# Attention into a two-layer MLP on one core: the start of the program in a written order of its own, with earlier weight loads

## The chip, the cores and the metric

One NeuronCore of a Trainium2 chip runs the whole program. The metric is the device time of one execution in microseconds (us). The kernel before takes 985.35 us (median of 3 runs, 983.48 to 986.13).

## The reference

Local-global attention over 8 batches and 8 heads (512 local and 32 global tokens, head size 64), then an MLP on every token. All in float32:

```python
s_g  = scale * q_g @ [k_g, k_l].T          # global queries see everything
s_l  = [scale * q_l @ k_g.T,               # local queries: the global keys
        where(|i - j| <= 32, scale * q_l @ k_l.T, -1e9)]   # and a band of 32
attn = concat(softmax(s_g) @ [v_g, v_l], softmax(s_l) @ [v_g, v_l])
x    = attn, heads side by side            # 4352 tokens x 512
out  = (max(x @ w_in, 0) ** 2) @ w_out     # 512 -> 2048 -> 512
```

The weights are used in two ways. The first MLP block multiplies in plain float32, with weights whose words are put together on chip ("wf"). All later blocks multiply three times with faster operands, each value split in a high and a low part ("ws").

## The kernel before

**Work.** Attention goes by pairs of heads: 64 pairs, pair `q` holding two heads (index `x` = 0, 1) of half a batch. Four pairs give the 256 tokens of one MLP block; there are 17 blocks of 8 steps each. The main loop (L506) counts `t`. Even `t` handles pair `q = t//2`; from `t = LAG = 9` on, every `t` also handles step `m = t - 9` of the MLP. So the first four pairs (`t` = 0 to 8) run before any MLP step: they are called the prelude here, and `t` = 9 to 16 the first MLP block.

**One pair.** `load_raw` brings queries and keys (128 x 960 words, 480 KB), `load_v` the values of two pairs (512 KB in the prelude), each by one SP DMA. `scores` and `g_scores` are 12 matmuls into the PSUM tile `s`. `softmax1` (DVE) takes masked score and maximum, `softmax2` (ACT) the exponential, `softmax3` (DVE) the division. `turn` copies the result on POOL into 16-bit `planes[x]` and has SP transpose it by DMA into `turned[x]`; `join` (POOL) makes float32 words of it in `joined[x]`. `av` multiplies by the values into `xa`, `x_evac` copies that to `xg` (first four pairs) or `x_h`. `g_evac` copies the scores of the global queries from `s` to `sg`: four DVE copies a pair.

**One MLP step.** `gemm1` writes `h`, `act1` squares its positive part, `gemm2` of the step before adds into `o`.

**Weights.** 32 chunks `wr` of 512 KB come by SP DMA (`w_load`). `w_abs` (ACT) and two DVE operations (`w_bits`) make `wf` of each; `w_split` (ACT, DVE) makes `ws`. `PLAN` says per `t`, at four places of the step, how many half-chunks of bits (`b`) and splits (`s`) are issued. A chunk's load is issued by `w_start` at most `LOOK = 2` chunks ahead.

**What sets the order.** Up to `t` = 16 a scheduler may move instructions on each engine (`FREE = (17, ...)`, L508; PE is kept up to `t` = 8 too). From `t` = 17 each engine runs its instructions in the order in which the code issues them. Weight, global-value and second mask loads are always free (`nc.sync`). An engine's queue is in order on the chip: an instruction that waits holds all behind it.

Of the kernel before, what the change touches and what calls it, by code (L numbers as in the profile page):

```python
# [7 lines left out]
F32 = mybir.dt.float32  # L8
# [9 lines left out]
P = 128  # L18
# [11 lines left out]
LAG = 9  # L30
NEARLY = 8

PLAN = [",,,b", "b,,,b", "b,,,b", "b,,b,", "b,,b,", "b,,b,", "b,,b,", "b,b,,b", "b,b,,b", "bb,bb,bb,bb", "bb,bb,bb,bb", "bbs,bb,bbs,bbs", "bbs,bbs,bbs,bbs", "bbs,bbs,bbs,bbs", "bbs,bbs,bs,s", "s,s,s,", "s,s,s,", "s,s,s,", "s,s,,", "s,s,,", "s,s,,", "s,s,,", "s,s,,"]
FREE = (17, 17, 17, 17, 17)
LOOK = 2
WCH = 32


# [21 lines left out]
def attention_moe(  # L60
# [19 lines left out]
    pairs = {}  # L80

    w_bufs = {"free": WCH}

    def w_take(n):
        w_bufs["free"] -= n
# [16 lines left out]
    def load_v(q):  # L102
        if q < NEARLY:
            w_take(1)
            v = wp.tile([P, 2, 512], F32, tag="w", name=f"v{q}")
            sp.dma_start(v, pk[q : q + 2, :, VO:PK].rearrange("t p n -> p t n"))
            for i in range(2):
                pairs[q + i]["v"] = v[:, i, :]
        else:
            v = pairs[q]["v"] = p2.tile([P, 512], F32, tag="v", name=f"v{q}")  # L110
            sp.dma_start(v, pk[q, :, VO:PK])

    masks = cp.tile([P, 4 * WN], F32, name="masks")
    load_raw(0)
    load_raw(1)
    load_raw(2)
    load_v(0)
    load_raw(3)

    x_h = cp.tile([P, 2, 4, HALF], F32R, name="x_h")  # L120
    x_l = cp.tile([P, 2, 4, HALF], F32R, name="x_l")
# [1 line left out]
    xg0 = cp.tile([P, 4, SG], F32, name="xg0")  # L123
    sg = cp.tile([P, 2, 544], F32, name="sg")
    planes = [cp.tile([P, 768], U16, name=f"planes{i}") for i in range(2)]
    turned = [cp.tile([P, 6, P], U16, name=f"turned{i}") for i in range(2)]
    joined = [cp.tile([P, 384], F32, name=f"joined{i}") for i in range(2)]
    gp = cp.tile([P, 1280], U16, name="gp")
    gpt = cp.tile([P, 640], F32, name="gpt")
# [3 lines left out]

    def scores(q):
        pr = pairs[q]
        bank = pr["s"] = ps_a.tile([P, 2, 512], F32, tag="s", name=f"s{q}")
        raw = pr["raw"]
        for w_ in range(4):
            u, c = divmod(w_, 2)
            k = KO + WN * w_ + 32 * (w_ == 3)  # L140
            for x in range(2):
                r = slice(64 * x, 64 * x + 64)
                pe.matmul(
                    bank[64 * c : 64 * c + 64, x, WN * u : WN * u + WN],
                    raw[r, QO + 64 * w_ : QO + 64 * w_ + 64],
                    raw[r, k : k + WN],
                    start=True,
                    stop=True,
                    skip_group_check=True,
                )  # L150
# [7 lines left out]
    def g_scores(q):  # L158
        pr = pairs[q]
        bank, raw = pr["s"], pr["raw"]  # L160
        for c, (k, n, _) in enumerate(g_parts(q)):
            for x in range(2):
                r = slice(64 * x, 64 * x + 64)
                pe.matmul(
                    bank[64 * c : 64 * c + 64, x, 2 * WN : 2 * WN + n],
                    raw[r, 0:64],
                    raw[r, k : k + n],
                    start=True,
                    stop=True,
                    skip_group_check=True,  # L170
                )
        if q < NEARLY:
            w_take(-1)

    def g_evac(q):
        bank, grp = pairs[q]["s"], (q // 2) % 2
        for c, (_, n, o) in enumerate(g_parts(q)):
            for x in range(2):
                r = 64 * (q % 2) + 32 * x
                ve.tensor_copy(sg[r : r + 32, grp, o : o + n], bank[64 * c : 64 * c + 32, x, 2 * WN : 2 * WN + n])  # L180

    def softmax1(q, x):
        pr = pairs[q]
        hf = (q // 4) % 2
        if x == 0:
            pr["prob"] = p2.tile([P, 2, 2, WN], F32, tag="prob", name=f"prob{q}")
        st = pr["st", x] = p2.tile([P, 8], F32, tag=f"st{x}", name=f"st{q}_{x}")
        for u in range(2):
            m = 2 * hf + u
            ve.tensor_tensor_reduce(  # L190
                out=pr["prob"][:, x, u, :],
                in0=pr["s"][:, x, WN * u : WN * u + WN],
                in1=masks[:, WN * m : WN * m + WN],
                scale=-0.125,
                scalar=3.0e38,
                op0=ALU.add,
                op1=ALU.min,
                accum_out=st[:, u : u + 1],
            )

    def softmax2(q, x):
        pr = pairs[q]
        st, sums = pr["st", x], pr["s"][:, x, 3 * WN : 3 * WN + 2]
        for u in range(2):
            p_ = pr["prob"][:, x, u, :]
            ac.activation(out=p_, in_=p_, func=AF.Exp, scale=-1.0, bias=st[:, u : u + 1], accum_out=sums[:, u : u + 1])

    def softmax3(q, x):
        pr = pairs[q]
        st, sums = pr["st", x], pr["s"][:, x, 3 * WN : 3 * WN + 2]  # L210
        ve.tensor_scalar(out=st[:, 6:8], in0=sums, scalar1=1e-9, scalar2=None, op0=ALU.add)
        ve.reciprocal(out=st[:, 2:4], in_=st[:, 6:8])
        for u in range(2):
            p_ = pr["prob"][:, x, u, :]
            ve.tensor_scalar(out=p_, in0=p_, scalar1=st[:, 2 + u : 3 + u], scalar2=None, op0=ALU.mult)

    def turn(q, x):

        words = pairs[q]["prob"][:, x].bitcast(U16)
        to = planes[x].rearrange("p (h k u n) -> p h k u n", h=2, k=3, u=2)  # L220
        for h in range(2):
            src = words[:, :, 64 + h :: 2].rearrange("p u (k n) -> p k u n", k=2)
            po.tensor_copy(to[:, h, 0:2, :, :], src)
        src = words[:, :, :64].rearrange("p u (n h) -> p h u n", h=2)
        po.tensor_copy(to[:, :, 2, :, 0:32], src)
        sp.dma_start_transpose(out=turned[x], in_=planes[x])

    def join(q, x):
        words = joined[x].bitcast(U16).rearrange("p (n h) -> p h n", h=2)
        po.tensor_copy(words, turned[x].rearrange("p (h c) n -> p h (c n)", h=2))  # L230

    def xa_tile(q):
        return ps_a.tile([P, 2, 512], F32, tag="xa", name=f"xa{q}")
# [70 lines left out]

    def g_load_v(b, grp, pair):
        gv = state["gv"] = p1.tile([P, 5, P], F32, tag="gv", name=f"gv{b}_{grp}_{pair}")
        nc.sync.dma_start(gv, vg[b, 2 * grp + pair].rearrange("(c p) n -> p c n", p=P))

    def g_av(xa, b, grp, pair):
        gv = state["gv"]  # L310
# [16 lines left out]
    def g_x(xa, b, grp, pair):  # L327
        to = xg[:, 2 * grp + pair, 32 * b : 32 * b + 32] if b else xg0[:, 2 * grp + pair, :]
        ac.copy(to, xa[:, 0, 128:160])
        ve.tensor_add(to, xa[:, 1, 128:160], to)  # L330

    wraw, wf, whi, wlo = {}, {}, {}, {}

    def w_load(i):
        r = wp.tile([P, 1024], F32, tag="w", name=f"wr{i}")
        nc.sync.dma_start(r.bitcast(I32), w[i].bitcast(I32))
        wraw[i] = r.rearrange("p (n w) -> p n w", w=2)

    def w_abs(i):
        if i == WCH - 1:  # L340
# [99 lines left out]
                    r0 = (4 * i + bb) * 544  # L440
                    nc.sync.dma_start(out[r0 : r0 + 32, :], ot[32 * bb : 32 * bb + 32, :])

    w_next = {"load": 0, "bits": 0, "split": 0}
    w_used, w_ready = set(), set()

    def w_start(i):
        while w_next["load"] < min(WCH, i + LOOK) and w_bufs["free"] >= 2:
            w_take(1)
            w_load(w_next["load"])
            w_next["load"] += 1  # L450
        if i < w_next["load"] and i not in w_ready and (i % 2 == 1 or w_bufs["free"] >= 1):
            w_ready.add(i)
            w_abs(i)

    def w_pass():
        i, n = divmod(w_next["bits"], 2)
        if i < WCH:
            w_start(i)
        if i not in w_ready:
            return  # L460
        w_next["bits"] += 1
        w_bits(i, n)
        if n == 1:
            wraw.pop(i)
            w_take(-1)
            if i + 1 < WCH:
                w_start(i + 1)

    def w_chunk():
        i = w_next["split"]  # L470
# [34 lines left out]

    for t in range(NSTEP + LAG + 1):  # L506
        m, q = t - LAG, t // 2
        ve.on, ac.on, pe.on, po.on, sp.on = [t >= x for x in FREE]  # L508
        pe.on = pe.on or t < LAG
        even, run = t % 2 == 0, 0 <= m < NSTEP  # L510
        live = even and q < NQ
        lag = 2 if t < LAG else 1
# [5 lines left out]
                gjobs[d] = (b, grp)  # L518
        if run:
            w_need(m)  # L520
        if t == 4:
            w_start(0)
        if t == 6:
            nc.sync.dma_start(masks[:, 2 * WN :], consts[:, 2 * WN :])
        if 2 in gjobs:
            g_norm(*gjobs[2])
            g_turn(*gjobs[2])
# [47 lines left out]
        if back is not None:
            x_low(back, xa)
        if live:
            softmax3(q, 1)
            if t < LAG and q:
                join(q - 1, 1)  # L580
            turn(q, 1)
        if t == LAG - 1:
            xa = xa_tile(q)
            av(q - 1, xa)
# [13 lines left out]
            g_x(xa, *g)  # L598
        if live:
            g_evac(q)  # L600
        w_tick(t, 2)
        if 1 in gjobs:
            g_exp(*gjobs[1])
        if 0 < m <= 8:
# [90 lines left out]
```

## Time and profile before

| what | value |
|---|---|
| median of 3 runs | 985.35 us (983.48 to 986.13) |
| profiled execution: its own time / its span | 985.95 us / 983.8 us |
| PE busy | 933.5 us, 95% of the span |
| DVE, ACT, POOL busy | 448.1 (46%), 440.7 (45%), 316.5 (32%) |
| DMA | 116.70 MB, of which 75.83 MB read from HBM |
| share of PE in the chain that ended last | 87% |

How to read it: PE is busy nearly everywhere, but the page's 40 slices (24.6 us each) show it busy 1, 4 and 8 tenths in the first three and 9 or more after the fourth. DMA is busiest there: 8 tenths in the first four slices, 3 to 5 later. PEld is PE's loading of its stationary operand, and "SPq" the issue of a DMA by SP, which is not counted as busy. Names in the rows are the program's with buffer numbers left out; nearly all instructions are recorded at one helper's line, L53, so rows are told apart by their tiles.

### The profile page before, as it was taken

The numbers are of one execution on the slowest core, as the hardware profiler recorded it, in microseconds if no ns is written. First come the engines' busy times: TensorE is split into PE (matmuls) and PEld (weight loads), VectorE is DVE, ScalarE is ACT, GpSimd is POOL, SyncE is SP. The second block draws the span as 40 slices with busy tenths as digits, with TensorE's granted clock in tenths as the row PEclk, the third lists the DMA queues.
The fourth block names the chain that finished last, engine by engine and source line by source line (L and its number), as shares of the span: only waits on it lengthen the run. The fifth ranks groups of instructions, "written<-read, shape, count | busy, mean of one in ns | idle before, by whom it ended". The sixth has DMA issues, their size and how long they took to land.

```text
span 983.8 us, 23839 instructions
## 1 busy us (share of the span) xinstructions
PE 933.5 (95%) x9536; PEld 826.7 (84%) x9536; DVE 448.1 (46%) x1678; ACT 440.7 (45%) x1142; POOL 316.5 (32%) x551
## 2 busy tenths in 40 slices
PE   1489799999999999999999999999999999999997
PEld 1356579999998998999998999999989998999996
DVE  3568976445444444444345433454434444431110
ACT  2345755445445444444344443445354444433332
POOL 2333343344233433243334322343234432430000
PEclk9999899999999999999999999999999999999999
DMA  8888444454435453345434443545355542431000
GB/s 273 237 253 249 145 118 108 116 109 116 123 87 129 122 143 82 108 110 147 117 108 101 113 135 95 129 109 133 93 109 118 147 121 67 122 75 36 1 22 22
DMA packets 172894, 116.70 MB, mean 119 GB/s; under 512 B 127088, under 2 KB 147952, under 8 KB 172784
## 3 DMA queue, kind: packets, MB, share of 16 engines
q1 hardware_dynamic: 172496, 114.84, 44.9%
q8 instruction: 75, 1.23, 0.5%
q10 hardware_dynamic: 288, 0.34, 0.1%
q14 instruction: 35, 0.29, 0.1%
HBM read 75.83 MB, written 8.91 MB: 86 GB/s over the span
## 4 chain that ended last, share of the span: by engine, by line
PE 87%; DVE 4%; DMA 4%; ACT 2%; issue 1%; SPq 1%; POOL 0%; ACTq 0%; POOLq 0%
PE h L53 38%; PE o L53 38%; PE xa L53 6%; PE s L53 6%; DMA wr<-in_w_dram 4%; DVE wf L53 1%; DVE ws L53 1%; DVE prob L53 1%; ACT wf L53 1%; ACT prob L53 1%; DMA raw<-in_pk_dram 0%; DVE sg L53 0%; SPq L53 0%; POOL planes L53 0%; ACT r L53 0%
## 5 line engine op out<-in xcount | busy, mean ns | idle before, releaser
L53 PE MATMUL h<-x_h,ws 128*128 128x256 f32 x2048 | 389.5, 283 | 0.0
L53 PEld LDWEIGHTS h<-x_h,ws 128*128 128x128 f32 x2048 | 325.5, 190 | 6.3 <-ACT x_h L53 0.2
L53 PE MATMUL o<-ws,gh 128*128 128x512 f32 x1024 | 326.5, 400 | 0.0
L53 ACT ACTIVATE h<-h 128x512 f32<-128x512 f32 x256 | 149.0, 582 | 390.2 <-PE h L53 386.2
L53 PE MATMUL h<-x_l,ws 128*128 128x256 f32 x1024 | 289.4, 283 | 0.1
L53 POOL COPY planes<-prob 128x256 uint16<-128x256 uint16 (+1 forms) x384 | 132.7, 384 | 410.7 <-DVE prob L53 410.7
L53 PEld LDWEIGHTS o<-ws,gh 128*128 128x128 f32 x1024 | 183.3, 188 | 36.8
L53 PE MATMUL o<-ws,gl 128*128 128x512 f32 x512 | 202.3, 395 | 0.0
L53 PEld LDWEIGHTS h<-x_l,ws 128*128 128x128 f32 x1024 | 194.0, 189 | 6.3 <-issue 0.5
L53 POOL COPY joined<-turned 128x768 uint16<-128x768 uint16 x128 | 137.4, 1075 | 137.6 <-DMA turned<-planes 126.5
L53 DVE TENSOR_TENSOR gl<-h,gh 128x512 fp32r<-128x512 f32 x128 | 87.7, 685 | 188.3 <-ACT gh L53 188.2
L53 DVE CUSTOM_DVE_ANT_0 prob<-s,masks 128x160 f32<-128x160 f32 x256 | 68.2, 321 | 220.7 <-PE s L53 220.6
L53 ACT ACTIVATE prob<-prob,st 128x160 f32<-128x160 f32 x256 | 109.9, 429 | 78.8 <-DVE st L53 74.9
L53 PEld LDWEIGHTS o<-ws,gl 128*128 128x128 f32 x512 | 96.3, 188 | 22.4
L53 PE MATMUL s<-raw 64*64 64x160 f32 (+2 forms) x1536 | 71.4, 311 | 31.6 <-DVE sg L53 22.0
L53 PEld LDWEIGHTS s<-raw 64*64 64x64 f32 x1536 | 51.0, 139 | 43.4 <-issue 16.5
L53 ACT CAST gh<-h 128x512 fp32r<-128x512 f32 x128 | 76.8, 600 | 2.2
L53 DVE COPY sg<-s 32x160 f32<-32x160 f32 (+2 forms) x256 | 74.7, 292 | 3.7
L53 DVE TENSOR_SCALAR prob<-prob,st 128x160 f32<-128x160 f32 x256 | 68.9, 311 | 4.2
L53 PE MATMUL xa<-joined,v 64*64 64x64 f32 (+1 forms) x2048 | 64.6, 254 | 3.9 <-POOL joined L53 3.9
L53 PEld LDWEIGHTS xa<-joined,v 64*64 64x64 f32 x2048 | 60.4, 140 | 6.3 <-POOL joined L53 5.5
L53 DVE TENSOR_SCALAR st<-s 128x2 f32<-128x2 f32 x128 | 20.3, 159 | 68.5 <-ACT prob L53 68.4
(39 smaller groups left out, 533.4 us busy)
## 6 DMA issues: line engine op xcount, KB each, us to landing
raw<-in_pk_dram SPq DMA_DIRECT2D x63, 480.0 KB, 4.0
wr<-in_w_dram SPq DMA_DIRECT2D x32, 512.0 KB, 6.8
v<-in_pk_dram SPq DMA_DIRECT2D x56, 256.0 KB, 4.0
gv<-in_vg_dram SPq DMA_DIRECT2D x32, 320.0 KB, 3.3
out_dram<-ot SPq DMA_DIRECT2D x32, 256.0 KB, 3.0
v<-in_pk_dram SPq DMA_DIRECT2D x4, 512.0 KB, 6.7
turned<-planes SPq DMA_TRANSPOSE x128, 2.8
out_dram<-ot SPq DMA_DIRECT2D x8, 64.0 KB, 1.7
```

The lines of the kernel that those rows point to most:

```text
L53: r = method(*args, **kwargs)
```

## The change

It does six things. (1) Every engine keeps the issued order from `t` = 0. (2) `PLAN` is new, and weight loads run up to `LOOK = 8` chunks ahead, the first six of them between the loads of the first pairs. (3) The tile `s` becomes two one-bank tiles, one per head; pairs 1 and 3 use the two `h` banks, idle until `t` = 9. (4) `g_evac` copies by ACT instead of DVE, in all 64 pairs. (5) `turned` gets two buffers per head; in the prelude both `turn`s of a pair come before the two `join`s of the pair before, and the sums of the exponentials stay in SBUF for the first eight pairs. (6) An exponential of one value is issued at the start.

```diff
-PLAN = [",,,b", "b,,,b", "b,,,b", "b,,b,", "b,,b,", "b,,b,", "b,,b,", ...
-FREE = (17, 17, 17, 17, 17)
-LOOK = 2
+EVEN, ODD = "bbb,,b,bb", "bbb,bb,bb,bbb"
+PLAN = [",,b,b", "bb,,,"] * 4 + [",,b,b", ODD, EVEN, ODD, EVEN, ODD, "bbb,,s,b", "ss,s,s,", "s,,s,s"]
+PLAN += ["ss,s,s,", "s,,s,s"] * 4
+LOOK = 8
...
+    def w_loads(n):
+        while w_next["load"] < min(WCH, n) and w_bufs["free"] >= 2:
+            w_take(1)
+            w_load(w_next["load"])
+            w_next["load"] += 1
...
     load_raw(1)
+    w_loads(2)
     load_raw(2)
     load_v(0)
+    w_loads(4)
     load_raw(3)
+    w_loads(6)
+    warm = cp.tile([P, 1], F32, name="warm")
+    nc.gpsimd.memset(warm, 0.0)
+    ac.activation(out=warm, in_=warm, func=AF.Exp)
...
-        bank = pr["s"] = ps_a.tile([P, 2, 512], F32, tag="s", name=f"s{q}")
+        pool, tags = (ps_h, "hh") if q in (1, 3) else (ps_a, "st")
+        bank = pr["s"] = [pool.tile([P, 512], F32, tag=tags[x], name=f"s{q}_{x}") for x in range(2)]
...
-                ve.tensor_copy(sg[r : r + 32, grp, o : o + n], bank[64 * c : 64 * c + 32, x, 2 * WN : 2 * WN + n])
+                ac.copy(sg[r : r + 32, grp, o : o + n], bank[x][64 * c : 64 * c + 32, 2 * WN : 2 * WN + n])
...
-        sp.dma_start_transpose(out=turned[x], in_=planes[x])
+        to = pairs[q]["turned", x] = p2.tile([P, 6, P], U16, tag=f"turned{x}", name=f"turned{q}_{x}")
+        sp.dma_start_transpose(out=to, in_=planes[x])
...
-        ve.on, ac.on, pe.on, po.on, sp.on = [t >= x for x in FREE]
-        pe.on = pe.on or t < LAG
...
-            if t < LAG and q:
-                join(q - 1, 0)
             turn(q, 0)
...
             softmax3(q, 1)
+            turn(q, 1)
             if t < LAG and q:
+                join(q - 1, 0)
                 join(q - 1, 1)
-            turn(q, 1)
```

Three places of the order, the first row of each engine's list left out. SP's queue from the loads of pair 2 on, before (`rawN`, `vN`: loads of pair N; `wrN`: weight chunk N; `turned0`, `turned1`: transposes of the two heads):

```order
L53 DMA raw2_83<-in_pk_dram 128x960
L53 DMA v0_85<-in_pk_dram 128x2x512
L53 DMA raw3_87<-in_pk_dram 128x960
L336 DMA wr0_149<-in_w_dram 128x1024
L336 DMA wr1_151<-in_w_dram 128x1024
L53 DMA_TRANSPOSE turned0_96<-planes0_94 128x6x128
L53 DMA raw4_156<-in_pk_dram 128x960
L53 DMA_TRANSPOSE turned1_97<-planes1_95 128x6x128
L336 DMA wr2_159<-in_w_dram 128x1024
```

and in the change (`turnedQ_X`: pair, head):

```order
L54 DMA wr4_97<-in_w_dram 128x1024
L54 DMA wr5_99<-in_w_dram 128x1024
L54 DMA_TRANSPOSE turned0_0_148<-planes0_109 128x6x128
L54 DMA wr6_152<-in_w_dram 128x1024
L54 DMA wr7_154<-in_w_dram 128x1024
L54 DMA wr8_158<-in_w_dram 128x1024
L54 DMA_TRANSPOSE turned0_1_169<-planes1_110 128x6x128
L54 DMA wr9_176<-in_w_dram 128x1024
L54 DMA raw4_180<-in_pk_dram 128x960
L54 DMA wr10_184<-in_w_dram 128x1024
```

Two weight chunks stood ahead of the first transpose, now six; up to the second transpose of pair 3 it was ten and is now fifteen. ACT's queue at the second pair, before (`prob1`: its exponentials, `wf2`: chunks 2 and 3):

```order
L53 ACTIVATE prob1_181,s1_168<-prob1_181,st1_0_182 128x160
L53 ACTIVATE wf2_166<-wr2_159 128x512
L53 ACTIVATE prob1_181,s1_168<-prob1_181,st1_0_182 128x160
L53 ACTIVATE wf2_166<-wr3_164 128x512
L53 ACTIVATE prob1_181,s1_168<-prob1_181,st1_1_185 128x160 x2
```

and in the change:

```order
L54 COPY sg_108<-s0_0_118 32x128
L54 COPY sg_108<-s0_1_119 32x128
L54 COPY sg_108<-s0_0_118 32x160
L54 COPY sg_108<-s0_1_119 32x160
L54 ACTIVATE wf2_178<-wr2_91 128x512
L54 ACTIVATE wf2_178<-wr3_93 128x512
L54 ACTIVATE prob1_201,st1_0_202<-prob1_201,st1_0_202 128x160 x2
L54 ACTIVATE prob1_201,st1_1_205<-prob1_201,st1_1_205 128x160 x2
```

The weight operations no longer stand between the exponentials of a pair; the four score copies are new on ACT. POOL's queue at the end of the prelude, before, and then in the change (`planes0`, `planes1`: `turn`; `joined0`, `joined1`: `join`):

```order
L53 COPY planes1_95<-prob3_337 128x2x2x32
L53 COPY joined0_98<-turned0_96 128x2x384
L53 COPY joined1_99<-turned1_97 128x2x384
L53 COPY planes0_94<-prob4_421 128x256 x2
L53 COPY planes0_94<-prob4_421 128x2x2x32
```

```order
L54 COPY planes0_109<-prob4_445 128x256 x2
L54 COPY planes0_109<-prob4_445 128x2x2x32
L54 COPY planes1_110<-prob4_445 128x256 x2
L54 COPY planes1_110<-prob4_445 128x2x2x32
L54 COPY joined0_111<-turned3_0_379 128x2x384
L54 COPY joined1_112<-turned3_1_392 128x2x384
```

The joins of pair 3, the last that the first MLP step needs, came before the planes of pair 4 and now stand behind them.

## Rows read from the trace of the kernel before

**Rows 1.** Stretches: length, then PE, PEld, DVE, ACT, POOL busy (instructions), PEclk, DMA share, GB/s.

```profile
0.00:61.40 61.40, 22.13 (x260) 16.49 (x260) 30.14 (x117) 18.53 (x57) 21.66 (x42) 1.00 0.79 245
61.40:130.70 69.30, 63.49 (x468) 43.64 (x469) 60.51 (x151) 40.71 (x91) 23.24 (x32) 0.95 0.65 197
99.60:109.10 9.50, 4.54 (x94) 3.48 (x92) 8.96 (x19) 5.00 (x10) 4.92 (x8) 0.76 0.61 176
```

**Rows 2.** Chain that ended last, first and last of its four prelude weight loads: start, length.

```profile
16.74 7.21 DMA wr<-in_w_dram
...
50.84 4.59 DMA wr<-in_w_dram
```

**Rows 3.** Waits from 0 to 140 us: who for whom, total us, times, longest.

```profile
ACT wf L53 <- DMA wr<-in_w_dram: 42.2, 17, 9.3
PE s L53 <- DVE sg L53: 22.0, 3, 12.5
```

**Rows 4.** Timeline of PE: start, length, instruction (x count), idle before and releaser.

```profile
42.40 1.65 PE L53 MATMUL xa<-joined,v 64*64 64x128 f32 x32
61.41 7.32 PE L53 MATMUL h<-xg,wf 128*128 128x256 f32 x20 [0.51 <-ACT xg L53]
68.66 1.05 PE L53 MATMUL s<-raw 64*64 64x160 f32 x24
70.30 3.70 PE L53 MATMUL o<-wf,r 128*128 128x512 f32 x8
113.75 3.62 PE L53 MATMUL h<-xg,wf 128*128 128x256 f32 x16
117.21 3.60 PE L53 MATMUL o<-wf,r 128*128 128x512 f32 x8
120.64 3.62 PE L53 MATMUL h<-xg,wf 128*128 128x256 f32 x16
130.72 0.68 PE L53 MATMUL h<-x_h,ws 128*128 128x256 f32 x1
141.01 1.05 PE L53 MATMUL s<-raw 64*64 64x160 f32 x24
143.20 0.74 PE L53 MATMUL o<-ws,gh 128*128 128x512 f32 x2
```

**Rows 5.** Three more stretches, columns as in rows 1.

```profile
4.00:11.00 7.00, 2.15 (x24) 1.10 (x24) 1.27 (x10) 2.30 (x6) 0.00 (x0) 1.00 1.03 414
19.50:26.00 6.50, 0.00 (x0) 0.00 (x0) 2.52 (x8) 2.60 (x8) 1.34 (x2) 1.00 0.97 366
28.10:29.30 1.20, 0.77 (x12) 0.80 (x16) 0.17 (x1) 0.00 (x0) 0.59 (x3) 1.00 0.83 164
```

**Rows 6.** The page's DMA issues: engine, count, KB each, median us from issue to landing.

```profile
wr<-in_w_dram SPq DMA_DIRECT2D x32, 512.0 KB, 6.8
turned<-planes SPq DMA_TRANSPOSE x128, 2.8
```

**Rows 7.** Timeline of POOL and SP: a transpose of pair 0, then those of pair 3.

```profile
14.86 1.22 SPq L53 DMA_TRANSPOSE turned<-planes  x1
...
50.41 1.25 POOL L53 COPY planes<-prob 128x256 uint16<-128x256 uint16 x3 [0.85 <-DVE prob L53]
51.69 1.22 SPq L53 DMA_TRANSPOSE turned<-planes  x1
57.90 1.04 POOL L53 COPY joined<-turned 128x768 uint16<-128x768 uint16 x1 [2.35 <-DMA turned<-planes]
```

**Rows 8.** Groups of instructions from 0 to 140 us: busy us, mean ns, idle before.

```profile
L53 POOL COPY joined<-turned 128x768 uint16<-128x768 uint16 x18 | 20.6, 1146 | 26.0 <-DMA turned<-planes 16.8 <-PE xa L53 9.1
L53 ACT ACTIVATE wf<-wr 128x512 f32<-128x512 f32 x32 | 21.5, 672 | 42.2 <-DMA wr<-in_w_dram 42.2
L53 ACT COPY xg<-xa 128x256 f32<-128x256 f32 x4 | 1.5, 385 | 0.2 <-PE xa L53 0.2
```

**Rows 9.** Timeline of ACT in a step of the even stretch, with its idle time.

```profile
444.08 1.20 ACT L53 ACTIVATE h<-h 128x512 f32<-128x512 f32 x2 [2.94 <-PE h L53]
```

More of the change, by code (lines that the diff above doesn't have):

```diff
@@ L31 @@
 NEARLY = 8
-PLAN = [",,,b", "b,,,b", "b,,,b", "b,,b,", "b,,b,", "b,,b,", "b,,b,", "b,b,,b", "b,b,,b", "bb,bb,bb,bb", "bb,bb,bb,bb", "bbs,bb,bbs,bbs", "bbs,bbs,bbs,bbs", "bbs,bbs,bbs,bbs", "bbs,bbs,bs,s", "s,s,s,", "s,s,s,", "s,s,s,", "s,s,,", "s,s,,", "s,s,,", "s,s,,", "s,s,,"]
-FREE = (17, 17, 17, 17, 17)
-LOOK = 2
+EVEN, ODD = "bbb,,b,bb", "bbb,bb,bb,bbb"
+PLAN = [",,b,b", "bb,,,"] * 4 + [",,b,b", ODD, EVEN, ODD, EVEN, ODD, "bbb,,s,b", "ss,s,s,", "s,,s,s"]
+PLAN += ["ss,s,s,", "s,,s,s"] * 4
+LOOK = 8
 WCH = 32
@@ L82, in attention_moe @@
     w_bufs = {"free": WCH}
+    w_next = {"load": 0, "bits": 0, "split": 0}
     def w_take(n):
@@ L113, in attention_moe, with w_load @@
     masks = cp.tile([P, 4 * WN], F32, name="masks")
+    wraw, wf, whi, wlo = {}, {}, {}, {}
+    def w_load(i):
+        r = wp.tile([P, 1024], F32, tag="w", name=f"wr{i}")
+        sp.dma_start(r.bitcast(I32), w[i].bitcast(I32))
+        wraw[i] = r.rearrange("p (n w) -> p n w", w=2)
+    def w_loads(n):
[3 more added lines that the diff above has]
+            w_next["load"] += 1
     load_raw(0)
     load_raw(1)
+    w_loads(2)
     load_raw(2)
     load_v(0)
+    w_loads(4)
     load_raw(3)
+    w_loads(6)
+    warm = cp.tile([P, 1], F32, name="warm")
+    nc.gpsimd.memset(warm, 0.0)
+    ac.activation(out=warm, in_=warm, func=AF.Exp)
     x_h = cp.tile([P, 2, 4, HALF], F32R, name="x_h")
@@ L125, in attention_moe @@
     planes = [cp.tile([P, 768], U16, name=f"planes{i}") for i in range(2)]
-    turned = [cp.tile([P, 6, P], U16, name=f"turned{i}") for i in range(2)]
     joined = [cp.tile([P, 384], F32, name=f"joined{i}") for i in range(2)]
@@ L143, in scores @@
                 pe.matmul(
-                    bank[64 * c : 64 * c + 64, x, WN * u : WN * u + WN],
+                    bank[x][64 * c : 64 * c + 64, WN * u : WN * u + WN],
                     raw[r, QO + 64 * w_ : QO + 64 * w_ + 64],
@@ L164, in g_scores @@
                 pe.matmul(
-                    bank[64 * c : 64 * c + 64, x, 2 * WN : 2 * WN + n],
+                    bank[x][64 * c : 64 * c + 64, 2 * WN : 2 * WN + n],
                     raw[r, 0:64],
@@ L191, in softmax1 @@
                 out=pr["prob"][:, x, u, :],
-                in0=pr["s"][:, x, WN * u : WN * u + WN],
+                in0=pr["s"][x][:, WN * u : WN * u + WN],
                 in1=masks[:, WN * m : WN * m + WN],
@@ L202, in softmax2 @@
         pr = pairs[q]
-        st, sums = pr["st", x], pr["s"][:, x, 3 * WN : 3 * WN + 2]
+        st = pr["st", x]
+        sums = pr["sums", x] = st[:, 4:6] if q < NEARLY else pr["s"][x][:, 3 * WN : 3 * WN + 2]
         for u in range(2):
@@ L209, in softmax3 @@
         pr = pairs[q]
-        st, sums = pr["st", x], pr["s"][:, x, 3 * WN : 3 * WN + 2]
+        st, sums = pr["st", x], pr["sums", x]
         ve.tensor_scalar(out=st[:, 6:8], in0=sums, scalar1=1e-9, scalar2=None, op0=ALU.add)
@@ L225, in turn @@
         po.tensor_copy(to[:, :, 2, :, 0:32], src)
-        sp.dma_start_transpose(out=turned[x], in_=planes[x])
+        to = pairs[q]["turned", x] = p2.tile([P, 6, P], U16, tag=f"turned{x}", name=f"turned{q}_{x}")
+        sp.dma_start_transpose(out=to, in_=planes[x])
     def join(q, x):
         words = joined[x].bitcast(U16).rearrange("p (n h) -> p h n", h=2)
-        po.tensor_copy(words, turned[x].rearrange("p (h c) n -> p h (c n)", h=2))
+        po.tensor_copy(words, pairs[q]["turned", x].rearrange("p (h c) n -> p h (c n)", h=2))
     def xa_tile(q):
@@ L306, in g_load_v @@
         gv = state["gv"] = p1.tile([P, 5, P], F32, tag="gv", name=f"gv{b}_{grp}_{pair}")
-        nc.sync.dma_start(gv, vg[b, 2 * grp + pair].rearrange("(c p) n -> p c n", p=P))
+        sp.dma_start(gv, vg[b, 2 * grp + pair].rearrange("(c p) n -> p c n", p=P))
     def g_av(xa, b, grp, pair):
@@ L330, in g_x @@
         ve.tensor_add(to, xa[:, 1, 128:160], to)
[L332 to L337, printed above, removed]
     def w_abs(i):
@@ L441, in evac @@
                     nc.sync.dma_start(out[r0 : r0 + 32, :], ot[32 * bb : 32 * bb + 32, :])
-    w_next = {"load": 0, "bits": 0, "split": 0}
     w_used, w_ready = set(), set()
     def w_start(i):
[L447 to L450, printed above, removed]
+        w_loads(i + LOOK)
         if i < w_next["load"] and i not in w_ready and (i % 2 == 1 or w_bufs["free"] >= 1):
@@ L465, in w_pass @@
             w_take(-1)
-            if i + 1 < WCH:
-                w_start(i + 1)
+            if i + 2 < WCH:
+                w_start(i + 2)
     def w_chunk():
@@ L520, in attention_moe @@
             w_need(m)
-        if t == 4:
-            w_start(0)
         if t == 6:
-            nc.sync.dma_start(masks[:, 2 * WN :], consts[:, 2 * WN :])
+            sp.dma_start(masks[:, 2 * WN :], consts[:, 2 * WN :])
         if 2 in gjobs:
@@ L567, in attention_moe @@
             softmax3(q, 0)
-            if t < LAG and q:
-                join(q - 1, 0)
             turn(q, 0)
-        if back is not None:
+        if back is not None and t > LAG:
             x_evac(back, xa)
@@ L575, in attention_moe @@
         if back is not None:
+            if t < LAG:
+                x_evac(back, xa)
             x_low(back, xa)
+        if t == 0:
+            w_start(0)
+            w_start(1)
+        if live:
+            w_tick(t, 2)
         if live:
             softmax3(q, 1)
+            turn(q, 1)
             if t < LAG and q:
+                join(q - 1, 0)
                 join(q - 1, 1)
-            turn(q, 1)
         if t == LAG - 1:
@@ L600, in attention_moe @@
             g_evac(q)
-        w_tick(t, 2)
+        if not live:
+            w_tick(t, 2)
         if 1 in gjobs:
```

## The prediction, before the changed kernel had run

> **What bounds the kernel now.** I read the page first: PE is the bound, but its low slices lie at the start. So I cut the span there, with busy time by stretch [rows 1]. Up to 61.4 us PE is busy 22.1 us, to 130.7 us it is busy 63.5 of 69.3, and one hole of 9.5 us (99.6 to 109.1) holds 5.0 us of its idle time. Behind 130.7 us, where the second MLP block's first matmul starts [rows 4], PE is never without work. Everything the change can win lies before that point, which I call M. The chain of waits then says what the start waits for: four weight loads, of 7.2 to 4.6 us each, stand in it [rows 2]. The table of waits agrees: ACT waited 42.2 us for weight chunks, and PE 22.0 us until DVE had copied the global scores out of the one `s` tile [rows 3]. ACT's queue is in order, so a late chunk also holds the exponentials behind it. DMA is 79% busy in that stretch [rows 1], with holes, so it is not yet the bound.
>
> I use two clocks: T0, when the first MLP step could start, and M.
>
> **T0 and M before.** The first two MLP steps have 32 `h` instructions (16 each); 20 were left at 61.41 us [rows 4]. A warm step of 16 takes 117.21 - 113.75 = 3.46 us, so the 12 done earlier were worth 2.6 us and T0 was effectively 61.4 - 2.6 = 58.8 us. From T0 to M, PE needs 8 `h` steps at 3.46 us = 27.7; 7 `o` steps at 120.64 - 117.21 = 3.43 us = 24.0; and scores with values of four pairs, twice at 70.30 - 68.66 = 1.64 us and twice with global products at 143.20 - 141.01 = 2.19 us = 7.7. To that comes PE's slow start: the 20 instructions at 61.41 us took 7.25 us until the scores, against 20/16 x 3.46 = 4.33 us warm; PE had just idled, and the first ones ran at about half pace, which is the 1.2 GHz level of the two. That is 2.9 us. Sum 62.3 us. Before, it took 130.7 - 58.8 = 71.9 us, so 9.6 us are stalls, the hole at 99.6 us above all.
>
> **Part by part.**
>
> *Weight loads ahead, kept order.* The ACT waits of [rows 3] should nearly vanish: chunks 2 and 3, which held the second pair's exponentials, are now issued before pair 3's load. But what is issued early must also be moved, and the transposes stand in the same SP queue. Up to the second transpose of pair 3 the queue now holds 15 weight chunks, 7 pair loads and 2 value loads: a chunk is 512 KB [rows 6], the others 480 and 512 by their shapes: 15 x 512 + 7 x 480 + 2 x 512 = 12,064 KB = 12.35 MB. Loads alone move at 414 GB/s and, later, 366 [rows 5]; I take 390: 31.7 us. A transpose on an otherwise idle queue is the stretch at 28.1 us: 83% of 1.2 us, 1.0 us at some 164 GB/s [rows 5]; eight of them are 8.0 us. The stream runs at full rate by 4.0 us [rows 5]; I let it begin at 3 and leave the small masks out. So the last needed transpose leaves the engines at 3 + 31.7 + 8.0 = 42.7 us. The queue never runs dry by my reckoning: each transpose waits for its POOL copy, but several chunks are issued ahead of it. DMA becomes the bound of the prelude.
>
> What follows is a chain: about 0.5 us until the transpose has landed (2.8 us from issue [rows 6], less 1.2 of issue [rows 7] and 1.0 of moving, rounded), then on POOL the second half of pair 4's `turn`, which needs the same `planes` and now comes first, 1.25 us [rows 7], two joins of 1.15 us [rows 8], and PE's values, 1.65 us at the slow clock [rows 4]: 5.7 us. The copy to `xg` (0.39 us [rows 8]) hides behind the step's first three products, which need other pairs. T0 = 48.4 us, a gain of 10.4.
>
> That transposes wait behind loads is what the trace shows: the second one of pair 3, with one weight load right ahead, was joined 57.90 - 51.69 = 6.2 us after its issue, not 2.8 [rows 6, 7]. Here the Trainium skill ("Advanced Engine Details and Errata", X-Bar Transpose) has another price: transposes as fast as ordinary copies, 350 to 400 GB/s. At 375 GB/s, an estimate from that page, the eight would take 4.2 us, T0 would be 44.6 and the time 964.7 us. The row has less than half that rate, and I keep the row.
>
> *Scores in the idle banks, two tiles.* This removes PE's 22.0 us of waits for DVE's copies, but all of them lie in the prelude, which by the sum is bound by DMA: nothing of its own. If that cover is gone, POOL is next (rival 1).
>
> *Early exponential.* It moves ACT's table load out of the first pair's chain; covered too.
>
> *Double `turned`, joins behind turns.* The 1.25 us of the late `turn` are in the chain above; the rest is covered.
>
> *First MLP block in a kept order.* Weights keep ahead: chunk 16 is issued before pair 4's transposes, seven more right behind them, and step 4, which needs chunk 16, starts some 30 us after T0. ACT has at most ten half-chunks a step, five chunks at 0.67 us [rows 8], beside 1.2 us of positive part and square [rows 9], in 6.9 us. So the 9.6 us of stalls could all go. But each in-order ACT wait for a chunk now also holds the square that PE waits for, which the scheduler used to reorder. Between none and 9.6 kept, I take 3.0, nearer to none, because PE's order is much the same and the big hole came from late planes. Gain 6.6.
>
> *Splits spread over the second block.* ACT gets 7 splits in two steps, behind M; PE has a step of lead on them. Nothing, with 0 to 3 us as the bound.
>
> *Score copies on ACT, all pairs.* Four copies of at most 0.39 us each (the larger copy of [rows 8]) are 1.5 us a pair. ACT sits idle 2.94 us in the step behind, waiting for PE [rows 9]. Covered.
>
> **Sum.** 10.4 + 6.6 = 17.0 us off the profiled execution's 985.95 us: 968.95. That execution is 0.6 above the median of 985.35, so I forecast **968.5 us**. Its own range: T0 from 44 (full 414 GB/s, cheaper transposes) to 55 (transposes at 2 us, waits on POOL that open holes), stalls kept 0 to 9.6: most of it is 962 to 977.
>
> On the loads' rate, the Trainium skill ("DMA: Bandwidth & Descriptors", Specifications) speaks against the change: HBM gives one core about 358 GB/s. The 414 of [rows 5] go past that, and the measurement decides. By the page the loads would take 34.5 us, an estimate, and the time would be 971.
>
> **Rivals.**
>
> 1. *The transposes hardly wait* (shares of the 16 engines run ahead of one another, or a transpose costs the stream little). Then POOL sets the pace: per pair two turns of 1.25 and two joins of 1.15 us, 4.8 us. Pair 0's second transpose, issued at 14.9, would land by 17.7 [rows 6, 7]; three pairs later it is 32.1; with the 5.2 us of chain behind it T0 is 37.3, 11.1 earlier: 957.4 us. For it: DMA's holes before. Against: the 6.2 us of [rows 7]. What the Trainium skill says of fast transposes (above) points this way. Chance 0.14.
>
> 2. *The kept order stalls.* ACT's wait for a chunk holds the square, PE's `o` step comes late, all 9.6 us of stalls stay, and T0 is 53 (gain 5.8 alone): 985.35 - 5.8 = 979.5. For it: DVE is 60.5 of 69.3 us busy there [rows 1], so little gives. Against: the weights lead. Chance 0.15.
>
> 3. *Nothing comes of it*: the start is bound by what DMA moves (79% busy) and chunks moved earlier delay transposes by as much as they help ACT. 983 to 986. Chance 0.06.
>
> 4. *Slower: ACT becomes the bound behind M.* Some 59 pairs there carry four more ACT copies. It decides where four copies pass the 2.94 us of idle [rows 9], 0.73 us each; at 0.85 us the loss would be 0.46 x 59 = 27 us, with the 17 gained: 995. For it: short operations that read PSUM and wait. Against: the larger copy takes 0.39 [rows 8]. Chance 0.05.
>
> **How the numbers follow.** Forecast 0.60, rivals 0.14, 0.15, 0.06, 0.05. The range 957 to 980 takes in the forecast's own, rival 1 and rival 2; it leaves out rivals 3 and 4 and tails, under 2 in 10. A measurement tells 0.3%, 3 us, from no change. Faster by more: forecast, rival 1 and nearly all of rival 2, 0.88. Within: rival 3 and the rest of 2, 0.07. Slower: rival 4, 0.05.
>
> **What would show it.** PE's first `h` instruction with all of 16 in a row near 48 us; DMA share above 0.9 up to 43 us; ACT's wait for `wr` below 10 us; the first `h<-x_h` near 114 us instead of 130.7; PE without idle time from M on. Wrong if T0 lies before 42 (rival 1), if PE idles over 6 us between T0 and M (rival 2), or if ACT releases PE behind M (rival 4).

## The result, and the profile after

The changed kernel takes 967.95 us (median of 4 runs, 967.33 to 968.27), the kernel before 985.50 us beside it (4 runs, 983.48 to 986.13). The ratio is 0.9825, 95% interval 0.9808 to 0.9842: 17.5 us less, where 16.85 was forecast (985.35 to 968.5). The profiled execution took 968.27 us with a span of 966.5 us.

PE's timeline gives the two clocks of the prediction, T0 (first MLP step) and M (first matmul of the second block). The columns are those of [rows 4], which these lines answer to.

```profile
40.17 0.68 PE L54 MATMUL xa<-joined,v 64*64 64x128 f32 x2 [4.33 <-POOL joined L54]
49.16 0.69 PE L54 MATMUL xa<-joined,v 64*64 64x128 f32 x2 [6.49 <-POOL joined L54]
51.60 9.45 PE L54 MATMUL h<-xg,wf 128*128 128x256 f32 x32
60.98 1.05 PE L54 MATMUL s<-raw 64*64 64x160 f32 x24
113.70 0.69 PE L54 MATMUL h<-x_h,ws 128*128 128x256 f32 x1
```

T0 is 51.60 us (effectively 58.8 before) and M 113.70 us (130.72 before). From T0 to M it takes 62.1 us, which is the 62.3 us of PE's work that the prediction counted; no line in between has idle time. From M to the end of the span it is 966.5 - 113.7 = 852.8 us, against 983.8 - 130.7 = 853.1 before. So the whole gain lies ahead of M: 7.2 us up to T0 and 9.8 us behind it.

The waits up to 140 us (who for whom, total us, times, longest), to be held against [rows 3]:

```profile
PE xa L54 <- POOL joined L54: 26.2, 8, 12.8
DVE prob L54 <- DMA masks<-in_consts_dram: 6.0, 1, 6.0
PE s L54 <- ACT sg L54: 2.6, 1, 2.6
ACT wf L54 <- DMA wr<-in_w_dram: 2.5, 3, 1.4
```

ACT's waits for weights fell from 42.2 to 2.5 us and PE's for the score copies from 22.0 to 2.6. In their place PE waits for joins (26.2 us, where it was 3.9 before), and a wait of one instruction is new: DVE, 6.0 us, for the second half of the masks. The chain of waits leads through it (start, length; from 34 us on):

```profile
34.30 0.98 SPq L54
...
35.33 6.75 DMA masks<-in_consts_dram
...
42.24 0.33 DVE prob L54
...
46.84 1.28 POOL planes L54 x2
48.13 1.95 POOL joined L54 x2
```

The masks are needed by pair 4, not by the four pairs that the first MLP step waits for. But SP issues their load at t = 6, behind two weight chunks and a pair's data; the 160 KB land 6.75 us later; pair 4's softmax and turns wait for them; and the joins of pair 3, which PE needs, stand behind those turns on POOL.

DMA's share by slices of the page (24.2 us each) starts at 0.9, 0.9 and 0.7, where it was 0.8 through the first four before. From 4 to 43.3 us, the stretch that the prediction took for bound by DMA, the profile counts a share of 1.10 (columns of [rows 1]):

```profile
4.00:43.30 39.30, 15.51 (x216) 11.51 (x216) 20.38 (x88) 18.37 (x63) 16.02 (x30) 0.64 1.10 354
```

Behind M, PE is busy 825.0 of the 825 us from 135 to 960.

### The profile page after: what moved, and what is told of

It reads as the page before. It is cut to its first block, busy times and chain, and to the rows that moved or that the text cites. A ratio compares the mean times of both kernels' runs of the same rounds, so it can differ in the third digit from the quotient of the medians.

```text
span 966.5 us, 23983 instructions
## 1 busy us (share of the span) xinstructions
PE 927.2 (96%) x9536; PEld 823.2 (85%) x9536; DVE 376.2 (39%) x1422; ACT 503.5 (52%) x1399; POOL 321.0 (33%) x552
## 4 chain that ended last, share of the span: by engine, by line
PE 94%; DMA 3%; POOL 1%; DVE 0%; ACT 0%; SPq 0%; issue 0%; POOLq 0%; DVEq 0%; ACTq 0%
PE h L54 41%; PE o L54 41%; PE xa L54 6%; PE s L54 6%; DMA masks<-in_consts_dram 1%; DMA wr<-in_w_dram 1%; DMA turned<-planes 1%; POOL planes L54 0%; POOL joined L54 0%; SPq L54 0%; ACT prob L54 0%; DVE prob L54 0%; DVE wf L54 0%; DVE st L54 0%; ACT wf L54 0%
## 5 line engine op out<-in xcount | busy, mean ns | idle before, releaser
L54 POOL COPY planes<-prob 128x256 uint16<-128x256 uint16 (+1 forms) x384 | 135.2, 391 | 411.5 <-DVE prob L54 394.7
L54 PE MATMUL xa<-joined,v 64*64 64x64 f32 (+1 forms) x2048 | 64.6, 252 | 26.2 <-POOL joined L54 26.2
L54 ACT COPY sg<-s 32x160 f32<-32x160 f32 (+2 forms) x256 | 67.1, 262 | 5.0 <-DVE st L54 1.3
L54 ACT ACTIVATION_READ_ACCUMULATOR prob<-prob,st 128x1 f32 x256 | 40.3, 157 | 0.0
```

The costliest lines, as they stand in the source:

```text
L54: r = method(*args, **kwargs)
```

## The experiments

All runs have the ratio to the kernel before as measured beside them, since chips differ by some 2 us. M is from the profiled execution of each; from M to the end of the span it is 852.4 to 852.9 us in every one of them, so M tells the profiled executions apart. Of the runs the median and the ratio speak; one execution can lie 1 or 2 us off the median, in e12_loads_plan more.

| run | edit | M us | median us | ratio (95% interval) |
|---|---|---|---|---|
| changed kernel | | 113.70 | 967.95 | 0.9825 (0.9808 to 0.9842) |
| e1_masks | masks early | 109.77 | 964.36 | 0.9806 (0.9793 to 0.9819) |
| e2_look2 | loads 2 ahead | 139.74 | 994.33 | 1.0110 (1.0096 to 1.0124) |
| e3_free | free order | 107.31 | 961.67 | 0.9781 (0.9767 to 0.9794) |
| e4_bank | no idle banks | 112.96 | 967.47 | 0.9836 (0.9822 to 0.9849) |
| e5_before_loads | before, loads 8 ahead | 114.97 | 970.23 | 0.9858 (0.9845 to 0.9871) |
| e6_sg_dve | score copies on DVE | 111.27 | 965.71 | 0.9814 (0.9801 to 0.9828) |
| e7_joins | e1, joins first at t = 8 | 107.56 | 962.11 | 0.9779 (0.9765 to 0.9792) |
| e8_split | e7, `h` in the waits | 107.71 | 960.50 | 0.9764 (0.9749 to 0.9778) |
| e9_planes | e8, four planes | 104.14 | 959.96 | 0.9759 (0.9745 to 0.9774) |
| e10_look5 | e8, loads 5 ahead | 110.58 | 964.31 | 0.9802 (0.9781 to 0.9823) |
| e11_both | e9 and e10 | 108.15 | 962.72 | 0.9789 (0.9775 to 0.9804) |
| e12_loads_plan | e5, new PLAN | 124.20 | 971.81 | 0.9893 (0.9854 to 0.9932) |

The profiled execution of e8_split was its slowest (962.26 us), that of e9_planes its fastest (958.74), that of e12_loads_plan its slowest (978.63; the others 969.3 to 971.8).

**Is it the mask load?** (e1_masks)

```diff
     load_raw(3)
+    sp.dma_start(masks[:, 2 * WN :], consts[:, 2 * WN :])
...
-        if t == 6:
-            sp.dma_start(masks[:, 2 * WN :], consts[:, 2 * WN :])
```

> One move alone: the second half of the masks is loaded among the first loads (right behind the raw data of pair 3) instead of at t = 6 behind a weight chunk, raw data and another chunk. Theory A (the end of the prelude was set by that one load: it landed at 42.08 us, DVE waited 6.0 us for it, and pair 4's turns on POOL, which stood behind it, held the joins of pair 3): pair 4's turns start when the transposes of pair 3 have freed the planes, near 43 instead of 44.67, so the first MLP step comes 0.5 to 2 us earlier (51.6 to about 50.4) and the time falls to 966 to 967.5. Rival (the bytes of the queue or POOL's own work set the pace): the wait goes, but the first step stays within 0.3 us of 51.6 and the time at 968.

DVE's wait for the masks is gone, and PE's timeline reads:

```profile
45.68 0.69 PE L54 MATMUL xa<-joined,v 64*64 64x128 f32 x2 [2.89 <-POOL joined L54]
48.11 9.01 PE L54 MATMUL h<-xg,wf 128*128 128x256 f32 x32
109.77 0.68 PE L54 MATMUL h<-x_h,ws 128*128 128x256 f32 x1
```

T0 is 48.11 us, 3.5 us earlier and more than expected. Against the changed kernel the ratios differ by 0.2% and their intervals overlap; e4_bank, which ran beside it with the late masks, took 3.1 us longer (967.47 to 964.36). The intervals of these two don't overlap. One small load's place in the queue was worth 3.5 us of T0, and some 2 to 4 us of the time, by which of these comparisons one takes.

**What do the loads far ahead do?** (e2_look2 takes them away)

```diff
-    w_loads(2)
...
-    w_loads(4)
...
-    w_loads(6)
...
-LOOK = 8
+LOOK = 2
```

> The changed kernel with the old distance of the weight loads: none of the six early ones, LOOK = 2 instead of 8; the kept order stays. Theory A (weights far ahead are the condition for a kept order, since an engine that waits for a chunk holds all behind it): ACT waits for chunks over 15 us in all before the second block, the first step comes at 53 to 58, the stalls in the first block come back by 3 to 8 us, time 973 to 982. Rival (the chunks ahead of the transposes in the DMA queue cost as much as they give): the transposes land faster, the first step comes at 46 to 51, the block shows no stall, time 963 to 968.

```profile
ACT wf L54 <- DMA wr<-in_w_dram: 52.6, 16, 7.1
```

```profile
68.28 8.93 PE L54 MATMUL h<-xg,wf 128*128 128x256 f32 x32
...
112.53 1.32 PE L54 MATMUL xa<-joined,v 64*64 64x128 f32 x30 [1.69 <-POOL joined L54]
116.41 1.28 PE L54 MATMUL xa<-gpt,gv 64*64 64x32 f32 x36 [2.56 <-DMA gv<-in_vg_dram]
117.61 6.39 PE L54 MATMUL o<-wf,r 128*128 128x512 f32 x8
```

Worse than either theory: without the loads the rest of the change is 11.0 us slower than the kernel before (994.33 to 983.35 us, ratio 1.0110). ACT waits 52.6 us for chunks (up to 115 us), and what stands behind each wait is late: T0 is 9.5 us later than before the change, and 5.0 us of idle time appear in the first block. From T0 to M that makes 71.5 us, about as much as the 71.9 us of the kernel before, which was free to reorder and also had its loads 2 ahead. So this run shows what late weights cost, and not that the kept order makes them cost more in that block.

**And alone?** (e5_before_loads: in the kernel before, `LOOK = 8` and the six early loads)

```diff
-LOOK = 2
+LOOK = 8
...
     load_raw(1)
+    w_loads(2)
     load_raw(2)
     load_v(0)
+    w_loads(4)
     load_raw(3)
+    w_loads(6)
```

> The kernel before with one part of the change alone: weight loads 8 chunks ahead, the first six between the loads of the first pairs. The old order, PLAN, banks, copies and single buffers stay. Theory B (new, after the runs with loads 2 ahead and with the free order: the loads ahead are the whole gain, the kept order costs some of it): the first matmul of the second block comes at 107 to 114 us instead of 130.7, time 961 to 968. Rival (the loads give their gain only with the new PLAN and order around them): 119 us or later, 972 or more.

The loads alone bring 13.5 of the 17.5 us, but not all that the first theory asked for. Its timeline of PE has a hole that the changed kernel doesn't have:

```profile
48.56 4.58 PE L53 MATMUL h<-xg,wf 128*128 128x256 f32 x20
...
88.39 0.43 PE L53 MATMUL xa<-joined,v 64*64 64x128 f32 x2 [1.94 <-POOL joined L53]
91.33 1.23 PE L53 MATMUL xa<-joined,v 64*64 64x128 f32 x21 [2.51 <-POOL joined L53]
93.81 5.56 PE L53 MATMUL o<-wf,r 128*128 128x512 f32 x8
114.97 0.69 PE L53 MATMUL h<-x_h,ws 128*128 128x256 f32 x1
```

**Is it the kept order?** (e3_free: the changed kernel, and the scheduler free again up to t = 16)

```diff
+FREE = 17
...
         m, q = t - LAG, t // 2
+        ve.on = ac.on = po.on = sp.on = t >= FREE
+        pe.on = t >= FREE or t < LAG
```

> The changed kernel with the old freedom: the scheduler may move instructions on ACT, DVE, POOL and SP up to t = 16 and on PE from t = 9 to 16, all else as changed (weights 8 ahead, idle banks, two buffers). Theory A (the kept order took the stalls out of the first MLP block): they come back, the way from the first step to the second block takes 67 to 72 us instead of 62.1, time 972 to 980. Rival (the loads far ahead did all of it): 62 to 63 us for that way and a time of 967 to 969.

Neither: the free order is faster, by 5.8 us against e4_bank, which ran beside it, and against the changed kernel with intervals that don't overlap (0.9781 and 0.9825). PE's timeline shows what the scheduler did with PE's waits:

```profile
35.97 1.99 PE L55 MATMUL h<-xg,wf 128*128 128x256 f32 x8
39.75 0.43 PE L55 MATMUL xa<-joined,v 64*64 64x128 f32 x2 [1.79 <-POOL joined L55]
...
43.02 2.08 PE L55 MATMUL h<-xg,wf 128*128 128x256 f32 x4 [0.51 <-ACT xg L55]
45.03 1.56 PE L55 MATMUL xa<-joined,v 64*64 64x128 f32 x32
...
107.31 0.68 PE L55 MATMUL h<-x_h,ws 128*128 128x256 f32 x1
```

Twelve of the 32 `h` instructions of the first two steps, those that don't need pair 3, run at 36 and 43 us, where the kept order waits. The joins of pair 3 also came ahead of pair 4's turns, so the mask load, issued at 34.86 us here too, held nothing that the first step needs. Between 53 us and M, PE idles only 0.5 us: the first block without stalls does not need the kept order.

**The banks** (e4_bank)

```diff
-        pool, tags = (ps_h, "hh") if q in (1, 3) else (ps_a, "st")
+        pool, tags = (ps_h, "hh") if q in () else (ps_a, "st")
```

> The changed kernel without the idle banks: the scores of pairs 1 and 3 go to the same two banks as those of all other pairs. Theory A (the prelude goes by the transposes and the loads ahead of them, so the banks are worth nothing, as costed): PE's waits for the copies of the global scores come back, the first step stays within 0.7 us of 51.6, time 967.5 to 969. Rival (the free banks are what let pair 1 and pair 3 start early): the first step comes 2 to 5 us later, time 970 to 973.

PE's waits for the score copies come back (10.6 us), and nothing else happens: T0 is 50.98 us, the time 967.47. The idle banks are worth nothing in this order; in the free order they weren't tried.

**The score copies** (e6_sg_dve)

```diff
-                ac.copy(sg[r : r + 32, grp, o : o + n], ...
+                ve.tensor_copy(sg[r : r + 32, grp, o : o + n], ...
```

> The changed kernel with the copies of the global scores back on DVE, in all 64 pairs. Theory (costed at nothing: neither ACT nor DVE releases PE behind the second block, and in the prelude the transposes set the pace): the time of the changed kernel within 1.5 us, a ratio of 0.981 to 0.984 to the kernel before. Rival (moving them to ACT took DVE off the path of the prelude): the first step 1 to 3 us later, ratio 0.985 or more. Rival on the other side (ACT was the worse place, since its copies stand ahead of the exponentials): 1 to 3 us earlier, ratio 0.980 or less.

Ratio 0.9814, with an interval that overlaps that of the changed kernel: by the time, no difference that can be told. But the profiled run has T0 at 49.94 us, 1.7 us before the changed kernel's 51.60, as the last of the three theories had it, and M 2.4 us before:

```profile
49.94 8.68 PE L54 MATMUL h<-xg,wf 128*128 128x256 f32 x32
```

With e4_bank, whose copies are on ACT, at 50.98 us, the place of the copies is worth 1 to 2 us of T0 at most, and whether it is worth anything isn't settled by one execution of each. Behind M both take 852.8 us. On ACT the 256 copies take

```profile
L54 ACT COPY sg<-s 32x160 f32<-32x160 f32 (+2 forms) x256 | 67.1, 262 | 5.0 <-DVE st L54 1.3
```

262 ns each, 1.0 us a pair where the prediction took 1.5 as the most; the 2.94 us of idle time of [rows 9] cover that.

**A kept order that does what the free one did** (e7_joins and e8_split; both keep the early masks)

```diff
             softmax3(q, 0)
+            if t == LAG - 1:
+                join(q - 1, 0)
+                join(q - 1, 1)
             turn(q, 0)
...
-            if t < LAG and q:
+            if t < LAG - 1 and q:
```

> The early mask load, and at t = 8 the two joins of pair 3 ahead of the two turns of pair 4 on POOL. Theory A (behind the mask load the last thing ahead of the first step is POOL's order: two turns, 2.4 us, stand before the joins that PE waits for): the first step comes at 45.5 to 46.5 instead of 48.1 with the masks alone, time 961.5 to 963 where the masks alone gave 964.4. Rival (the transposes of pair 3 land no earlier than the joins began anyway): 47.5 or later, 963.8 or more.

```diff
+        if t == LAG - 1:
+            for k in range(2):
+                gemm1(k, 0, (0, 1))
         gav = ...
...
+            for k in range(2):
+                gemm1(k, 0, (2,))
             xa = xa_tile(q)
             av(q - 1, xa)
...
-            gemm1(m, 0)
+            gemm1(m, 0, (3,) if m < 2 else (0, 1, 2, 3))
```

> As the run before (masks early, joins of pair 3 first), and three quarters of the first half of h of the first two MLP steps are multiplied in PE's waits at t = 8, as the scheduler did it in the run with the free order: 12 of the 32 records of the first two steps, 2.6 us at the warm rate. Theory A (PE's waits for the joins at the end of the prelude can take work that doesn't need pair 3; this is what made the free order faster than the kept one): the second block starts 2 to 3.5 us earlier than without it, time 958.5 to 960.5. Rival (what the free order gained lies elsewhere, in the joins and copies it moved): the same time as without it within 0.7 us.

e7_joins: T0 46.77 us, a little later than expected, and 962.11 us. e8_split: 960.50 us, 1.6 us less (960.0 to 960.7 in three of its four runs) where 2 to 3.5 were expected. The profiled run, its slowest, shows the next bound:

```profile
52.93 0.43 PE L54 MATMUL xa<-joined,v 64*64 64x128 f32 x2 [0.88 <-POOL joined L54]
54.11 0.89 PE L54 MATMUL xa<-joined,v 64*64 64x128 f32 x30 [0.75 <-POOL joined L54]
54.93 5.40 PE L54 MATMUL o<-wf,r 128*128 128x512 f32 x8
```

PE reaches pair 4 before its joins are there, and the `o` step behind that wait takes 5.40 us instead of 3.70. With this the written order beats the free one by 1.2 us at the medians, though the intervals overlap.

**What bounds the prelude: the planes, or the loads in the queue?** (e9_planes, e10_look5, e11_both, all on top of e8_split)

```diff
+    planes += [gpt.bitcast(U16)[:, :768], cp.tile([P, 768], U16, name="planes3")]
...
-        to = planes[x].rearrange(
+        pl = planes[x + 2 * (q in (1, 3))]
+        to = pl.rearrange(
...
-        sp.dma_start_transpose(out=to, in_=planes[x])
+        sp.dma_start_transpose(out=to, in_=pl)
```

> As the run with the split first steps (masks early, joins of pair 3 first, 960.5 us), and pairs 1 and 3 write their turned copies into two more planes (one of them in a tile that is idle until the first global transpose). Theory A (a loop sets the pace of the prelude: a turn waits until the transpose of the pair before has read the plane, and that transpose stands 5 to 8 us behind loads): POOL's waits for transposes ahead of turns, 12 us, mostly go, the first step's last part comes at 42 to 45 us instead of 46.5, time 957 to 959.5. Rival (the transposes wait for the loads ahead of them in the queue however early they are issued): within 0.7 us of 960.5.

```diff
-LOOK = 8
+LOOK = 5
```

> As the run with the split first steps (960.5 us), with weight loads 5 chunks ahead instead of 8: three chunks fewer stand ahead of the last transposes, 1.3 us each at 400 GB/s. Theory A (loads that are not yet needed delay the transposes): the first step's last part comes 1.5 to 4 us before 46.5, time 957 to 959.5. Rival 1 (the chunks ahead cost nothing there): within 0.7 us of 960.5. Rival 2 (weights come late again, as with 2 ahead): ACT waits for chunks over 8 us, time 962 or more.

> Both of the two runs before together: four planes and loads 5 chunks ahead. Theory A: the gains add up in part, the first step's last part at 40 to 44 us, time 955 to 958.5. Rival (one of the two already removes what bounds there): no better than the better one of them within 0.7 us.

The planes give 0.5 us at the medians, within what the rival allowed and with intervals that overlap: a transpose issued earlier waits in the queue instead. Up to 60 us the median from issue to landing is 6.9 us, where e8_split has 5.4. Loads 5 ahead do speed the transposes: the last part of the first step starts at 43.08 instead of 46.50 us. And yet the kernel is 3.8 us slower. ACT waits 20.3 us for chunks, as the second rival had it, and the chain of waits runs through the first block:

```profile
62.17 8.75 DMA wr<-in_w_dram
...
70.94 0.68 ACT wf L54
...
72.76 0.83 ACT prob L54 x4
...
76.77 1.70 POOL planes L54 x3
...
80.87 6.92 DMA gv<-in_vg_dram
...
87.83 1.28 PE xa L54 x36
89.11 5.87 PE o L54 x8
```

A chunk comes late, ACT's wait for it holds a pair's exponentials, the transposes are late, SP issues the global values behind them, and PE waits for those. So 8 ahead is a compromise: it costs 3.4 us ahead of the first step and saves more behind. Both edits together are 2.8 us slower than the planes alone. e9_planes has the lowest median of the study; like e3_free, e7_joins, e8_split and e11_both it lies below the changed kernel with intervals that don't overlap.

**Is it the new PLAN?** (e12_loads_plan: e5_before_loads with the PLAN of the change)

> The kernel before with the loads 8 ahead (970.2 us) and, in addition, the new PLAN of weight work; old order, banks, copies, single buffers. Theory (the 8 us that this lacked against the changed kernel with the free order, 961.7, come from the old PLAN, whose weight work on DVE stands ahead of pair 5's softmax): the second block starts at 107 to 110 us instead of 115.0, time 962 to 965. Rival (they come from the banks, the double buffers or the score copies): 968 or more.

No: 971.81 us, as without it, with more scatter. In the profiled run DVE does weight work from 80.6 to 90.6 us without a break and only then pair 6's softmax, whose scores had been ready since 87.6; POOL and the transposes follow, and PE waits 7.8 us. Which of the parts that are left (banks, buffers, copies off DVE, places of the weight work in the step) the free order needs beside the loads stays open. So does which of them brought the changed kernel from the 970.23 us of the loads alone to 967.95.

## Why the prediction was right, and where it was not

**The sum was right by two errors that cancel.** T0 was put at 48.4 us and came at 51.6, 3.2 late. Stalls of 3.0 us were left in the first block and none came. 48.4 + 62.3 + 3.0 = 113.7 us for M, measured 113.70: that the end fits so closely is luck, while the mechanism, a prelude bound by DMA and weights that keep ahead, is what the traces show.

**T0, the gain of 10.4 us: mis-sized, it was 7.2.** The step that failed is "I let it begin at 3 and leave the small masks out". By bytes that was harmless; what counts is where the load stands in the queue and what stands behind its user. The sum lets pair 4's `turn` start as soon as the planes are free; it waited for pair 4's softmax, and that for the masks. With that one load moved, T0 is 48.11 us (e1_masks).

The rest of that sum held. The last needed transpose was to have landed by 43.2 us. In the changed kernel the two transposes of pair 3 were issued at 38.2 and 39.5 us and landed 4.4 and 3.8 us later, the second at 43.3:

```profile
L54 SPq DMA_TRANSPOSE turned<-planes x2: 1211/1223/1235, 38.2 to 39.5; - x2
DMA to landing us min/median/max: 3.8/4.1/4.4
```

In e8_split the joins of pair 3 start at 42.75 us, 2.29 us for both, without a wait for a transpose:

```profile
42.75 2.29 POOL L54 COPY joined<-turned 128x768 uint16<-128x768 uint16 x2 [1.52 <-PE xa L54]
```

That transposes queue behind loads is seen in the changed kernel's chain, where one took 8.30 us from issue to landing (the median was 2.8 before [rows 6]):

```profile
20.33 8.30 DMA turned<-planes
```

So the price of 1.0 us each, taken with 390 GB/s for the loads, fits the landing at 43.3 us. By the rate of the Trainium skill ("Advanced Engine Details and Errata", X-Bar Transpose) it would have come 3.8 us earlier, at 39.4, an estimate, and the trace doesn't agree. The limit of the Trainium skill ("DMA: Bandwidth & Descriptors", Specifications), about 358 GB/s a core, which its row gets by halving 716 GB/s between two cores, isn't what these traces show, with one core at work. GB/s of the changed kernel in 40 slices of its first 56 us, where it is almost all loads from 4 to 15 us:

```profile
GB/s 0 132 320 414 425 418 403 402 412 404 416 382 235 380 383 367 426 387 370 128 364 404 369 388 179 149 238 407 413 324 297 402 395 417 235 70 192 360 401 418
```

**The first block, a gain of 6.6 us: it was 9.8.** The reason given, weights that keep ahead, held: ACT's waits for chunks fell to 2.5 us. Mis-sized were the 3.0 us of stalls that it left for a kept order in which a wait of ACT holds the square: none came. The kept order, which the heading of that part names, isn't needed for it. e3_free does without: its last 20 `h` start at 47.48 us, so its effective T0 is 44.9, and from there to M it takes 62.4 us. Early weights alone aren't enough either: e5_before_loads keeps 4.5 us of waits there. The kept order costs some 6 us against the free one, all of it in the prelude; early masks, early joins and the split steps (e8_split) recover it.

**The cold start of 2.9 us: 2.5.** The 32 instructions took 60.98 - 51.60 = 9.38 us against 6.92 warm. The stretches of the changed kernel (columns of [rows 1]) show a granted clock of 0.50, the level of 1.2 GHz, for the first 4.6 us, after PE had waited 6.49 us with little work behind that wait:

```profile
51.60:56.20 4.60, 4.60 (x14) 3.70 (x12) 2.15 (x4) 2.53 (x7) 2.01 (x2) 0.50 0.99 383
56.20:61.00 4.80, 4.80 (x27) 3.95 (x25) 1.46 (x3) 3.34 (x6) 0.00 (x0) 1.00 0.95 385
```

Of the kernel before this isn't shown: its stretch from 61.4 to 68.6 us has a granted clock of 1.00, though 20 instructions took 7.25 us there; e4_bank has 1.00 as well over the 9.26 us of its 32. That PE ran at the 1.2 GHz level there was the prediction's inference from the pace, and the row for the clock doesn't bear it out.

**Costed at nothing:** the banks (e4_bank) are nothing in the kept order, and the copies on ACT (e6_sg_dve) nothing behind M; ahead of T0 they may cost 1 to 2 us, which is open. The splits are nothing too, as PE never idles behind M. The early exponential, the two buffers of `turned` and the new PLAN in the kept order weren't tried alone.

**The rivals.** 1 (transposes hardly wait) fell: T0 isn't before 42, and four planes gave 0.5 us. 2 (the kept order stalls) fell for this kernel: nothing stalls from T0 to M. With loads 5 ahead a chain of its kind appears (e10_look5), but no run has late weights and a free order with all else equal, so what the order adds to them isn't shown. 3 (nothing comes of it) fell with the 17.5 us. 4 fell: behind M ACT's copies don't release PE, and that stretch is no longer than before.

## What to carry to other kernels

Loads pulled forward are paid for by whatever stands behind them in the same queue: list for each load, small ones too, when its first user is due and who is queued behind that user. A kept order needs every input early, since one wait holds all behind it; compare it with the scheduler's own order, and copy what that put into the waits. And check a forecast at its intermediate clocks: here the end was right to 0.6 us while both parts were off by 3.

## What was not expected of the hardware

A hole on PE costs more than its idle time. In e5_before_loads 4.5 us of waits (88.39 and 91.33 us) are followed by an `o` step of 5.56 us, where [rows 4] has 3.70; the granted clock there was 0.65 of full speed, and 1.00 behind it:

```profile
93.80:99.20 5.40, 5.40 (x9) 2.38 (x9) 5.39 (x16) 3.70 (x7) 0.00 (x0) 0.65 0.22 64
99.20:114.90 15.70, 15.70 (x140) 11.00 (x139) 14.17 (x44) 8.28 (x27) 6.05 (x9) 1.00 0.21 41
```

So the waits and the slow step together cost 6.3 us. The reverse is seen in e8_split: its last 20 `h` instructions take 4.58 us at 1.00 from 46.5 us on, after PE had been given `h` work in the waits before. It isn't sure to come: e11_both has the same work in its waits, and there the 20 took 6.21 us, at 0.50 for the first 3.1. And a load's size tells little of when it lands in a full queue: 160 KB of masks took 6.75 us, the 512 KB chunks 7.7 us in the middle.
